# First attention's 16-tile matrix product by seven block products, and two of the down weights' block sums moved one layer later

## The chip, the cores and the metric

The kernel runs on one core of a Trainium2 chip. The metric is device time in microseconds (us) for one execution. A core has a matrix engine (TensorE, "PE" in the profile, with its weight loads as "PEld"), a vector engine (VectorE, "DVE"), an activation engine (ScalarE, "ACT"), a general engine (GpSimd, "POOL") and a queue engine that issues most of the transfers (SyncE, "SP"). Matrix products are written to eight banks of PSUM, each 128 partitions by 512 floats; everything else lives in SBUF.

## The reference

Four layers run one after the other on a token matrix x of 2048 by 1024, each on a layer norm of x and each added back to x: attention, gated unit, attention, gated unit. The weights of both attentions are the same, and so are those of both gated units.

```python
def _A_ref(x, wqkv, wo):                       # x is the layer-normed xn; 32 heads of 32
    q, k, v = split(x @ wqkv)                  # each 2048 x 1024
    pq, pk = phi(q), phi(k)                    # phi(t) = (t + 1 if t > 0 else exp(t)) + 1e-6
    kv = einsum("bhsd,bhse->bhde", pk, v)      # per head, sum over the 2048 tokens
    z = einsum("bhsd->bhd", pk)
    o = einsum("bhqd,bhde->bhqe", pq, kv) / (einsum("bhqd,bhd->bhq", pq, z)[..., None] + 1e-6)
    return o @ wo

def _B_ref(x, W_gate, W_up, W_down):           # F = 3584
    return (relu(x @ W_gate) * (x @ W_up)) @ W_down
```

Layer 0 and layer 2 are the attentions, layer 1 and layer 3 the gated units.

## The kernel before

v is never computed for the tokens. Since v = xn Wv, the kernel forms M = xnᵀ pk (1024 by 1024, a sum over all 2048 tokens) and multiplies Wv onto it afterwards, only on the diagonal blocks of the heads. The tokens are 16 tiles of 128. In layer 0 the product M is done plainly: 8 slices of 128 rows by 2 halves of 512 columns, each a chain of 16 matmuls over the token tiles.

```python
def m_units(d):                                       # layer 0, d = 0..7
    mt = self.temp([P, D], BF16, name=f"mt{l}_{d}")
    for h in range(H):                                # 2 halves
        ps = self.ps3.tile([P, NW], F32, tag="b")
        for t in range(self.ST):                      # 16 token tiles, L473
            nc.tensor.matmul(ps, lhsT=self.xn[l, t][:, d * P:(d + 1) * P],
                             rhs=self.pk[l, t][:, h * NW:(h + 1) * NW], ...)
            ...
        nc.scalar.activation(out=mt[:, h * NW:(h + 1) * NW], in_=ps, func=ACT.Copy)
        if h == H - 1:
            later.at(2, lambda: kv_step(d, mt))       # 8 matmuls of 128 columns (L485)
        later.tick()
```

In layer 2 the same M is done by Strassen's seven products in Winograd's form. M is split into 2 by 2 blocks of 512 by 512, with the tokens split into tiles 0 to 7 and 8 to 15. Each product is 4 PSUM banks of 8 matmuls (L534). The block sums are written over the tokens' own tiles, in float16.

```python
def m_products(q_first):                              # layer 2 only; cut
    X = [4 banks of pool ps, tag "a"]; Y = [2 of ps3, tag "b"] + [2 of kvp]
    def product(A, B, banks, start, done):
        for j in range(QT):                           # 4 banks
            for i in range(NS):                       # 8 token tiles, L534
                nc.tensor.matmul(banks[j], lhsT=A(i)[:, j * P:(j + 1) * P], rhs=B(i), ...)
            done(j)
            later.tick()
    product(lambda i: half(xn(i), 0), lambda i: half(pk(i), 0), X, True, lambda j: copy(Y[j], X[j]))
    product(lambda i: half(xn(NS + i), 0), lambda i: half(pk(NS + i), 0), X, False, evict(X, 0, 0))
    z_row()
    later.at(2, lambda: z_chain(0))
    ...
    product(lambda i: part(i, 0), lambda i: part(i, 2), V, True, keep)
    product(lambda i: part(i, 1), lambda i: part(i, 3), Y, False, lambda j: add(V[j], j))
    product(lambda i: f16(half(xn(NS + i), 0)), lambda i: half(pk(NS + i), 1), V, False, evict(V, 0, 1))
    product(lambda i: f16(half(xn(i), 1)), lambda i: f16(half(pk(i), 1)), Y, False, ...)
    ...                                               # copies, kv steps, then the o0 weights' load
    product(lambda i: half(xn(NS + i), 1), lambda i: f16(half(pk(NS + i), 0)), Y, False, last)
    q_first(); steps(1, 0); ring.load_to(ring.index((l, "o1")) + 1); finish_kv()
```

Around M: the k projections (`project`, L436) end just before it, each followed by `phi`: on ACT an exp, on DVE a `tensor_scalar` (L383) and a `scalar_tensor_tensor` (L385) that reads the projection's PSUM bank and frees it. The pk are summed over the tokens on POOL (L455). Beside and after M runs the chain of the denominators, token tile by token tile: multiply on POOL (L611), reduce and reciprocal on DVE (L616 to L618), scale on POOL (L623), transpose by a DMA on the SP queue (L628). After M come the last quarter's q projections, interleaved with four `fold_wo` (L642), which put kv and Wo together into T, and then the output product (L657) and the residual add (L664).

The gated units' weights are used by Strassen sums as well. Those of the down weights are made in layer 0 and stored in device memory for all four uses:

```python
for i in range(self.U // 2):                          # 7 pairs, from layer 0's second quarter on
    later.at(1 + 8 * i, lambda i=i: self.make_d(2 * i))
def make_d(self, u):                                  # load 1 MB; 6 turns later 4 DVE sums of
    ...                                               # 128x1024 (L806 to L809); then store 1 MB
```

The gate and up weights' sums are made in layer 1's first half (`make_gu`, L789 to L792), right behind the last multiply of a unit (`put`, L862). `later.at(n, f)` runs f after n turns, a turn being one matmul chain. `slot()` takes one of 16 SBUF buffers of 8 KB per partition.

Of the kernel before, what the change touches and what calls it, by code (L numbers as in the profile page):

```python
# [14 lines left out]
P = 128  # L15
NW = 512
HD = 32
QT = 4
# [71 lines left out]
class _Net:  # L90
# [146 lines left out]
    def head(self):  # L237
# [5 lines left out]
        nc.vector.memset(zero, 0.0)  # L243
        idle = self.ps3.tile([P, NW], F32, tag="b")
        for _ in range(11):
            nc.tensor.matmul(idle, lhsT=zero[:, 0:P], rhs=zero, start=True, stop=True)

# [122 lines left out]
    def phi(self, ps, out, kind):  # L370

        nc = self.nc
        e = self.temp()
        if kind == "v":
            nc.scalar.activation(out=e, in_=ps, func=ACT.Exp)
        else:
            nc.scalar.activation(out=e, in_=ps, func=ACT.Relu, scale=-1.0)
            nc.scalar.activation(out=e, in_=e, func=ACT.Exp, scale=-1.0)
            nc.scalar.activation(out=e, in_=e, func=ACT.Identity, bias=self.eps6[:, 0:1])

        def join():
            if kind == "v":
                nc.vector.tensor_scalar(out=e, in0=e, scalar1=1.0, scalar2=1e-6, op0=ALU.min,  # L383
                                        op1=ALU.add)
            nc.vector.scalar_tensor_tensor(out=out, in0=ps, scalar=0.0, in1=e,  # L385
                                           op0=ALU.max, op1=ALU.add)

        if self.phi_lag:
            self.later.at(self.phi_lag, join)
        else:  # L390
            join()
# [17 lines left out]
    def layer_A(self, l, last_ln):  # L409
# [4 lines left out]
        pq_of, pqT, T = {}, {}, []  # L414
        kv = [] if l else [self.kvp.tile([P, NW], F32, tag=f"kv{i}", name=f"kv{l}_{i}")
                           for i in range(H)]
        kvc = self.slot(f"kvc{l}", [P, 4, D])
# [23 lines left out]
        def k_unit(q, j, c, between=None):  # L441
# [4 lines left out]
            if l and t >= self.NS and c == H - 1:  # L446
                later.at(3, lambda: sums_k(t - self.NS))

# [18 lines left out]

        def m_units(d):
            mt = self.temp([P, D], BF16, name=f"mt{l}_{d}")
            for h in range(H):  # L470
                ps = self.ps3.tile([P, NW], F32, tag="b")
                for t in range(self.ST):
                    nc.tensor.matmul(ps, lhsT=self.xn[l, t][:, d * P:(d + 1) * P],  # L473
                                     rhs=self.pk[l, t][:, h * NW:(h + 1) * NW],
                                     start=(t == 0), stop=(t == self.ST - 1))
                    if t == self.ST // 2 - 1:
                        later.tick()
                nc.scalar.activation(out=mt[:, h * NW:(h + 1) * NW], in_=ps, func=ACT.Copy)
                if h == H - 1:
                    later.at(2, lambda: kv_step(d, mt))  # L480
                later.tick()

        def kv_half(d, mt, b):
# [6 lines left out]

        def kv_step(d, mt):
            for b in range(H):
                kv_half(d, mt, b)
            if d == KT - 1:
                ring.free_before((l, "q0"))
                finish_kv()

        half = lambda a, n: a[:, n * NW:(n + 1) * NW]
        part = lambda i, k: half(self.x[self.NS + i][:, :].bitcast(F16), k)
        sub = lambda out, a, b: nc.vector.tensor_tensor(out=out, in0=a, in1=b, op=ALU.subtract)  # L500

        def sums_n(i):

            a, b = self.xn[l, i], self.xn[l, self.NS + i]
            nc.vector.tensor_tensor(out=part(i, 0), in0=half(a, 1), in1=half(b, 1), op=ALU.add)
            sub(part(i, 1), part(i, 0), half(a, 0))
            sub(half(a, 1).bitcast(F16), half(a, 0), half(a, 1))

        def sums_k(i):
            a, b = self.pk[l, i], self.pk[l, self.NS + i]  # L510
            sub(part(i, 2), half(a, 1), half(a, 0))
            sub(part(i, 3), half(b, 1), part(i, 2))
            sub(half(a, 1).bitcast(F16), half(b, 1), half(a, 1))

        def sums_last(i):
            a, b = self.xn[l, self.NS + i], self.pk[l, self.NS + i]
            sub(half(a, 0).bitcast(F16), half(a, 0), part(i, 1))
            sub(half(b, 0).bitcast(F16), half(b, 0), part(i, 3))

        def m_products(q_first):  # L520

            NS = self.NS
            xn, pk = (lambda i: self.xn[l, i]), (lambda i: self.pk[l, i])
            f16 = lambda a: a.bitcast(F16)
            copy = lambda out, src: nc.scalar.activation(out=out, in_=src, func=ACT.Copy)
            X = [self.ps.tile([P, NW], F32, tag="a", name=f"mx{j}") for j in range(QT)]
            Y = [self.ps3.tile([P, NW], F32, tag="b", name=f"my{j}") for j in range(2)]
            Y += [self.kvp.tile([P, NW], F32, tag=f"kv{j}", name=f"my{2 + j}") for j in range(2)]
            mt, V, M5 = [], [], []

            def product(A, B, banks, start, done):
# [23 lines left out]
            z_row()  # L555
            later.at(2, lambda: z_chain(0))
            V += [self.ps.tile([P, NW], F32, tag="a", name=f"mv{j}") for j in range(QT)]
            for i in range(NS):
                later.at(1 + i // 2, lambda i=i: sums_last(i))
            product(lambda i: part(i, 0), lambda i: part(i, 2), V, True, keep)  # L560
# [69 lines left out]
        def fold_wo(n):  # L630
# [14 lines left out]
            for i in range(R):  # L645
                g = a * R + i
                dst = T[g // 4][:, g % 4, n2 * NW:(n2 + 1) * NW]
                if l or g % 2:
                    nc.scalar.activation(out=dst, in_=ps[i], func=ACT.Copy)
                else:  # L650
                    nc.vector.tensor_copy(out=dst, in_=ps[i])

# [34 lines left out]
        for i in range(QT, self.ST):  # L687
            self.ln_at((8 if l == 0 else 2) + 3 * (i - QT), l, i, 2)
            if l and i >= self.NS:
                later.at(4 + 3 * (i - QT), lambda i=i: self.send_away(i))  # L690
                later.at(10 + 3 * (i - QT), lambda i=i: sums_n(i - self.NS))
        if l == 0:
# [15 lines left out]
        for q in range(1, self.NQ - 1):  # L708
            if (l, q) == (0, 1):
                for i in range(self.U // 2):  # L710
                    later.at(1 + 8 * i, lambda i=i: self.make_d(2 * i))
            run(row_major(k_unit, q), row_major(q_unit, q))
        run(row_major(k_unit, self.NQ - 1))
        with self.tc.manual_schedule(engines={mybir.EngineType.DVE, mybir.EngineType.Pool}):
            q3 = row_major(q_unit, self.NQ - 1)
            out0 = column_major(out_unit, 0)
            if l == 0:
                ring.free_before((l, "v0"))
                later.at(5, z_row)
                later.at(7, lambda: z_chain(0))  # L720
                for d in range(KT):
                    m_units(d)
            else:
                ring.load_to(ring.index((l, "v1")) + 1)
                m_products(q3.pop(0))
                q3.insert(0, lambda: None)
                later.at(1, lambda: self.behind(ring.last, self.bring_back, range(self.NS)))
                for t in range(self.NS, self.ST, 2):
                    later.at(10 + t, lambda t=t: self.behind(self.last_turn, self.bring_back, (t, t + 1)))

# [53 lines left out]
    def make_gu(self, t, w, u):  # L784
# [9 lines left out]
            out=self.tgu[w, u], in_=t[:, 4:8, :].bitcast(F16)))  # L794

    def make_d(self, u):

        v = self.nc.vector
        t = self.slot(f"wd{u}", [P, 2, 4, NW])
        T = t[:, :, :, :].bitcast(F16)  # L800
        us = slice(u, u + 2)
        self.nc.sync.dma_start(out=t[:, :, :, :].rearrange("p u (h n) f -> p u h (n f)", h=2),
                               in_=self.wd_v[:, :, us, :].rearrange("p h u n -> p u h n"))

        def sums():
            v.tensor_tensor(out=T[:, :, 0, :], in0=t[:, :, 1, :], in1=t[:, :, 0, :], op=ALU.subtract)  # L806
            v.tensor_tensor(out=T[:, :, 1, :], in0=t[:, :, 3, :], in1=t[:, :, 1, :], op=ALU.subtract)
            v.tensor_tensor(out=T[:, :, 3, :], in0=t[:, :, 3, :], in1=T[:, :, 0, :], op=ALU.subtract)
            v.tensor_tensor(out=T[:, :, 2, :], in0=t[:, :, 2, :], in1=T[:, :, 3, :], op=ALU.subtract)  # L809
            self.later.at(2, lambda: self.nc.sync.dma_start(  # L810
                out=self.td[:, us, :, :], in_=T))

        self.later.at(6, sums)

# [155 lines left out]
    def layer_B(self, l, final):  # L970
# [6 lines left out]
        for c in range(2):  # L977
            hT = []
            first = l == 1 and c == 0
            for u in range(self.U):  # L980
                if u % 2 == 0:
                    hT.append(self.slot(f"h{l}_{c}_{u // 2}", dtype=F16))
                ring.load_to(ring.index((l, c, "g", u)) + 5)
                if first:
                    if u + 1 < self.U:
                        self.later.at(4, lambda u=u: behind(self.last_put if u else self.last_x, lambda: [
                            self.make_gu(ring.get((l, c, w, u + 1)), w, u + 1) for w in "gu"]))
                self.glu(l, c, u, hT)
                if c == 0 and u == (self.U - 1 if first else 0):
# [74 lines left out]
```

## Time and profile before

| what | value |
|---|---|
| time, median of three | 1479.12 us (1478.75 to 1479.19) |
| span of the profiled execution | 1476.4 us |
| PE busy / DVE busy / ACT busy / POOL busy | 1468.0 / 864.9 / 518.9 / 283.8 us |
| granted TensorE clock | 1.00 |
| layer 0's k and q projections | 9.5 to 105 us |
| layer 0's M product | 105.6 to 167 us |
| layer 1, first half, gated units | about 237 to 407 us |
| layer 2's M product | 841 to 895 us |

A line of the grouped view gives source line, engine, operation, written and read buffers with their shapes and the count; then the total busy time and the mean of one. A line of the view of stages gives the stretch, then for each engine its busy time and, in brackets, its count of instructions. A line of the timeline gives the start in us, the duration, and what ran; in square brackets how long the engine had been idle and what ended it.

### The profile page before, as it was taken

To read this page: it belongs to the slowest core of one execution; us is meant where nothing else is said; L and a number is where in the kernel's file an instruction comes from. 1 tells how busy PE (TensorE), PEld (TensorE's weight loads), DVE (VectorE), ACT (ScalarE), POOL (GpSimd) and SP (SyncE) were. 2 spreads that over 40 slices of the span, in tenths; PEclk is the share of its full clock that TensorE was granted. 3 is DMA by queue.
4 is the path that set the end of the run, shared out by engine and by line. 5 is a ranking of instruction groups with operands and counts; after the bars stand their busy time and mean duration, and the time that the engine had idled before them with its cause. 6 is when DMAs were issued, how large, how long until landed. Compare 5 with 4: busy or idle time off the path is not lost.

```text
span 1476.4 us, 18611 instructions
## 1 busy us (share of the span) xinstructions
PE 1468.0 (99%) x6965; PEld 667.7 (45%) x7007; DVE 864.9 (59%) x1487; ACT 518.9 (35%) x931; POOL 283.8 (19%) x190
## 2 busy tenths in 40 slices
PE   9999999999999999999999999999999999999999
PEld 4444444444444444444444444444444444444444
DVE  8995788666594433346379866874435434343632
ACT  5762323333330233340057525333333203333300
POOL 1356640111100011110023476401111001111000
PEclk9999999999999999999999999999999999999999
DMA  9856539444458953445933019994444688444461
GB/s 283 213 169 178 122 57 250 157 143 157 160 178 239 344 176 129 149 131 187 288 101 72 1 33 257 255 283 143 143 143 149 179 249 258 143 145 147 151 206 43
DMA packets 316060, 251.33 MB, mean 170 GB/s; under 512 B 105536, under 2 KB 291136, under 8 KB 315072
## 3 DMA queue, kind: packets, MB, share of 16 engines
q1 hardware_dynamic: 306000, 229.80, 53.0%
q10 hardware_dynamic: 9968, 20.32, 3.6%
q8 instruction: 55, 0.90, 0.3%
q14 instruction: 37, 0.30, 0.1%
HBM read 190.84 MB, written 34.60 MB: 153 GB/s over the span
## 4 chain that ended last, share of the span: by engine, by line
PE 91%; DVE 2%; issue 1%; ACT 0%; DVEq 0%
PE yg L851 10%; PE yu L851 10%; PE dy L935 10%; PE ps L436 8%; PE ps L657 7%; PE dv L935 7%; PE dx L935 7%; PE xu L851 6%; PE xg L851 6%; PE ps L473 4%; PE vg L851 3%; PE zu L851 3%; PE zg L851 3%; PE vu L851 3%; PE my L534 1%; PE mv L534 1%
## 5 line engine op out<-in xcount | busy, mean ns | idle before, releaser
L851 PEld LDWEIGHTS <-w 128*128 128x128 f16 (+1 forms) x3136 | 306.5, 98 | 370.9 <-DVE w L789 0.9
L889 POOL TENSOR_TENSOR h<-m5u,m5g 128x512 f16<-128x512 f32 x56 | 71.2, 1271 | 809.5 <-DVE m5u L885 798.6
L436 PE MATMUL ps<-w,xnT 128*128 128x512 bf16 x1024 | 223.9, 379 | 0.5 <-DVE pq L385 0.2
L935 PEld LDWEIGHTS <-h 128*128 128x128 f16 x1120 | 109.6, 98 | 132.1
L882 DVE TENSOR_TENSOR zg<-yg,m5g 128x512 f32<-128x512 f32 x56 | 39.1, 699 | 202.3 <-PE yg L851 202.3
L436 PEld LDWEIGHTS <-xnT 128*128 128x128 bf16 x1024 | 99.4, 98 | 120.9 <-issue 2.8
L851 PE MATMUL xu<-xnT,w 128*128 128x512 f16 x448 | 115.3, 379 | 0.0
L851 PE MATMUL xg<-xnT,w 128*128 128x512 f16 x448 | 115.1, 379 | 0.0
L851 PE MATMUL yu<-s,w 128*128 128x512 f16 x448 | 115.0, 379 | 0.0
L851 PE MATMUL yg<-s,w 128*128 128x512 f16 x448 | 115.0, 379 | 0.0
L657 PE MATMUL ps<-T,pqT 128*128 128x512 bf16 x500 | 110.4, 379 | 0.6
L859 ACT ACTIVATE m5g<-m5g 128x512 f32<-128x512 f32 x56 | 35.2, 629 | 199.7 <-DVE m5g L885 199.7
L935 PE MATMUL dy<-w,h 128*128 128x512 f16 x448 | 98.0, 379 | 0.0
L935 PE MATMUL dx<-w,h 128*128 128x512 bf16 x436 | 96.7, 379 | 0.6
L611 POOL TENSOR_TENSOR kvc<-pq,kvc 128x1024 f32<-128x1024 bf16 x32 | 70.6, 2206 | 70.3 <-DVE den L616 56.2
L161 ACT ACTIVATE rstd<-mv,eps 128x1 f32<-128x1 f32 x64 | 18.2, 290 | 169.6 <-DVE mv L159 169.5
L154 DVE BATCH_NORM_STATS2 stats<-x 128x6 f32<-128x512 f32 (+1 forms) x120 | 76.5, 671 | 1.9 <-DMA x<-in_A_x_dram 1.7
L657 PEld LDWEIGHTS <-pqT 128*128 128x128 bf16 x512 | 49.9, 98 | 60.4 <-issue 0.5
L455 POOL TENSOR_TENSOR kvc<-kvc,slab 128x512 f32<-128x512 f32 x46 | 58.3, 1274 | 75.1 <-DVE slab L385 57.4
L862 DVE TENSOR_TENSOR h<-yu,r 128x512 f16<-128x512 f32 x56 | 38.7, 691 | 56.1 <-PE yu L851 56.1
L885 DVE TENSOR_TENSOR m5u<-yu,m5u 128x512 f32<-128x512 f32 x56 | 38.7, 691 | 54.3 <-PE yu L851 53.3
L935 PEld LDWEIGHTS <-e 128*128 128x128 f16 x448 | 43.8, 98 | 52.9
(127 smaller groups left out, 1967.7 us busy)
## 6 DMA issues: line engine op xcount, KB each, us to landing
w<-in_B_W_gate_dram SPq DMA_DIRECT2D x56, 512.0 KB, 6.0
w<-in_B_W_up_dram SPq DMA_DIRECT2D x56, 512.0 KB, 4.6
w<-td SPq DMA_DIRECT2D x32, 896.0 KB, 4.8
w<-in_B_W_down_dram SPq DMA_DIRECT2D x24, 896.0 KB, 5.3
w<-tg SPq DMA_DIRECT2D x42, 512.0 KB, 7.0
w<-tu SPq DMA_DIRECT2D x42, 512.0 KB, 5.8
w<-in_A_wqkv_dram SPq DMA_DIRECT2D x10, 1024.0 KB, 8.1
away<-x SPq DMA_DIRECT2D x16, 512.0 KB, 4.0
```

The source lines that it names most:

```text
L154: self.nc.vector.bn_stats(out=stats[:, c, :], in_=src[:, c * fmax:(c + 1) * fmax])
L436: nc.tensor.matmul(by_row(ps), lhsT=self.xnT[l, l_q][:, kt, j * P:(j + 1) * P], rhs=w[:, kt, :].rearrange("p (b i d) -> p i b d", i=R, d=H ...
L455: nc.gpsimd.tensor_tensor(out=ksum[:, cols], in0=ksum[:, cols], in1=pk, op=ALU.add)
L473: nc.tensor.matmul(ps, lhsT=self.xn[l, t][:, d * P:(d + 1) * P], rhs=self.pk[l, t][:, h * NW:(h + 1) * NW], start=(t == 0), stop=(t == sel ...
L611: nc.gpsimd.tensor_tensor(out=prod, in0=pq_of[sc, j], in1=zrow, op=ALU.mult)
L657: nc.tensor.matmul(ps, lhsT=pqT[sc][:, g, j * P:(j + 1) * P], rhs=T[g // 4][:, g % 4, n2 * NW:(n2 + 1) * NW], start=(g == 0), stop=(g == G ...
L851: nc.tensor.matmul(ps, lhsT=W[w][m][:, k, :], rhs=A[m][:, k, :], start=start and k == 0, stop=k == 3, skip_group_check=True)
L862: self.last_put = nc.vector.tensor_tensor(out=h[:, b, :], in0=ps, in1=R.pop(b), op=ALU.mult)
L882: nc.vector.tensor_tensor(out=Z[w], in0=Y[w], in1=V[w], op=ALU.add)
L885: nc.vector.tensor_tensor(out=V[w], in0=Y[w], in1=V[w], op=ALU.add)
L889: nc.gpsimd.tensor_tensor(out=h[:, 3, :], in0=V["u"], in1=V["g"], op=ALU.mult)
L935: nc.tensor.matmul(banks[j], lhsT=A(k)[:, j * P:(j + 1) * P], rhs=w[:, i, :], start=start and k == 0, stop=k == self.U - 1, skip_group_che ...
```

## The change

Layer 0 now takes the route of layer 2: `m_units` is removed, and `m_products` serves both attentions. What differs in layer 0 is where the block sums live and when they are made. They are written over the raw tokens, which layer 0 holds as bf16 in the upper half of each x tile (`self.xb`); so the raw tokens are loaded from device memory once more before the output product adds them. The sums are made by 64 DVE operations of 128x512, four for each turn, beginning with M's first product.

```diff
-        def m_units(d): ...
+        def part(i, k):
+            if l == 0:
+                return half(f16(self.xb[self.NS + i if k < 2 else i]), k % 2)
+            return half(self.x[self.NS + i][:, :].bitcast(F16), k)
+        n1 = lambda i: op(part(i, 0), half(xn(i), 1), half(xn(self.NS + i), 1), ALU.add)
+        n2 = lambda i: op(part(i, 1), part(i, 0), half(xn(i), 0))
+        ...                                      # n3, n4, and k1 to k4 likewise
+            if l == 0:
+                jobs = [(f, i) for fs in ((n1, k1), (n2, k2), (n3, k3), (n4,), (k4,))
+                        for i in range(NS) for f in fs]
+                for n, (f, i) in enumerate(jobs):
+                    later.at(1 + n // 4, lambda f=f, i=i: f(i))
-            later.at(2, lambda: z_chain(0))
+            later.at(2 if l else 8, lambda: z_chain(0))
@@ layer_A
-            if l == 0:
-                ring.free_before((l, "v0"))
-                later.at(5, z_row)
-                later.at(7, lambda: z_chain(0))
-                for d in range(KT):
-                    m_units(d)
-            else: ...
+            bring = self.bring_back if l else self.load_x
+            ring.load_to(ring.index((l, "v1")) + 1)
+            m_products(q3.pop(0))
+            q3.insert(0, lambda: None)
+            later.at(1, lambda: self.behind(ring.last, bring, range(self.NS)))
+            for t in range(self.NS, self.ST, 2):
+                later.at(10 + t, lambda t=t: self.behind(self.last_turn, bring, (t, t + 1)))
```

Smaller parts go with it. The PSUM banks of pool kvp, which layer 0's kv held, become free for the products and for the warm-up matmuls at the start. `phi`'s intermediate becomes bf16 where DVE finishes it, in both attentions. All of `fold_wo`'s copies go to ACT. Two of the seven pairs of down weights' sums leave layer 0 and are made in layer 1's first half, one DVE operation in each of the units 2 to 9.

```diff
-        idle = self.ps3.tile([P, NW], F32, tag="b")
+        idle = [self.kvp.tile([P, NW], F32, tag=f"kv{i}", name=f"idle{i}") for i in range(2)]
@@ phi
-        e = self.temp()
+        e = self.temp(dtype=BF16 if kind == "v" else F32)
@@ fold_wo
-                if l or g % 2:
-                    nc.scalar.activation(out=dst, in_=ps[i], func=ACT.Copy)
-                else:
-                    nc.vector.tensor_copy(out=dst, in_=ps[i])
+                nc.scalar.activation(out=dst, in_=ps[i], func=ACT.Copy)
@@ layer_A
-                for i in range(self.U // 2):
+                for i in range(self.U // 2 - 2):
                     later.at(1 + 8 * i, lambda i=i: self.make_d(2 * i))
@@ layer_B, in the units of layer 1's first half
+                    if u in (1, 5):
+                        d = self.U - 4 + u // 2
+                        wd[d] = self.load_d(d)
+                    if 1 < u < 10:
+                        self.later.at(4, lambda d=self.U - 4 + (u - 2) // 4 * 2, n=(u - 2) % 4: behind(
+                            self.last_put, lambda: self.sums_d(wd[d], d, (n,))))
```

The change is for fewer matmuls in layer 0's M product, with the sums' work on an engine that has time there.

More of the change, by code (lines that the diff above doesn't have):

```diff
@@ L243, in head @@
         nc.vector.memset(zero, 0.0)
-        idle = self.ps3.tile([P, NW], F32, tag="b")
-        for _ in range(11):
-            nc.tensor.matmul(idle, lhsT=zero[:, 0:P], rhs=zero, start=True, stop=True)
+        idle = [self.kvp.tile([P, NW], F32, tag=f"kv{i}", name=f"idle{i}") for i in range(2)]
+        for i in range(11):
+            nc.tensor.matmul(idle[i % 2], lhsT=zero[:, 0:P], rhs=zero, start=True, stop=True)
         k0, k1, v0, q0, q1 = (ring.place() for _ in range(5))
@@ L414, in layer_A @@
         pq_of, pqT, T = {}, {}, []
-        kv = [] if l else [self.kvp.tile([P, NW], F32, tag=f"kv{i}", name=f"kv{l}_{i}")
-                           for i in range(H)]
+        kv = []
         kvc = self.slot(f"kvc{l}", [P, 4, D])
@@ L446, in k_unit @@
             if l and t >= self.NS and c == H - 1:
-                later.at(3, lambda: sums_k(t - self.NS))
+                later.at(3, lambda: sums(t - self.NS, k1, k2, k3))
         def k_sum(t, cols):
@@ L465, in z_row @@
                 nc.scalar.activation(out=zrow[:, i * NW:(i + 1) * NW], in_=ps, func=ACT.Copy)
[L468 to L481, printed above, removed]
         def kv_half(d, mt, b):
@@ L489, in kv_half @@
                                  skip_group_check=True)
[L491 to L496, printed above, removed]
-        half = lambda a, n: a[:, n * NW:(n + 1) * NW]
[L499 to L518, printed above, removed]
+        half = lambda a, n: a[:, n * NW:(n + 1) * NW]
@@ new lines, in layer_A, with op @@
+        f16 = lambda a: a.bitcast(F16)
+        xn, pk = (lambda i: self.xn[l, i]), (lambda i: self.pk[l, i])
+        def part(i, k):
+            if l == 0:
+                return half(f16(self.xb[self.NS + i if k < 2 else i]), k % 2)
+            return half(self.x[self.NS + i][:, :].bitcast(F16), k)
+        def op(out, a, b, how=ALU.subtract):
+            nc.vector.tensor_tensor(out=out, in0=a, in1=b, op=how)
+        n1 = lambda i: op(part(i, 0), half(xn(i), 1), half(xn(self.NS + i), 1), ALU.add)
@@ new lines, in layer_A @@
+        n2 = lambda i: op(part(i, 1), part(i, 0), half(xn(i), 0))
+        n3 = lambda i: op(f16(half(xn(i), 1)), half(xn(i), 0), half(xn(i), 1))
+        n4 = lambda i: op(f16(half(xn(self.NS + i), 0)), half(xn(self.NS + i), 0), part(i, 1))
+        k1 = lambda i: op(part(i, 2), half(pk(i), 1), half(pk(i), 0))
+        k2 = lambda i: op(part(i, 3), half(pk(self.NS + i), 1), part(i, 2))
+        k3 = lambda i: op(f16(half(pk(i), 1)), half(pk(self.NS + i), 1), half(pk(i), 1))
+        k4 = lambda i: op(f16(half(pk(self.NS + i), 0)), half(pk(self.NS + i), 0), part(i, 3))
@@ L520, in m_products, with sums @@
+        def sums(i, *fs):
+            for f in fs:
+                f(i)
         def m_products(q_first):
             NS = self.NS
-            xn, pk = (lambda i: self.xn[l, i]), (lambda i: self.pk[l, i])
-            f16 = lambda a: a.bitcast(F16)
             copy = lambda out, src: nc.scalar.activation(out=out, in_=src, func=ACT.Copy)
@@ L555, in m_products @@
             z_row()
-            later.at(2, lambda: z_chain(0))
+            later.at(2 if l else 8, lambda: z_chain(0))
             V += [self.ps.tile([P, NW], F32, tag="a", name=f"mv{j}") for j in range(QT)]
-            for i in range(NS):
-                later.at(1 + i // 2, lambda i=i: sums_last(i))
+            if l:
+                for i in range(NS):
+                    later.at(1 + i // 2, lambda i=i: sums(i, n4, k4))
             product(lambda i: part(i, 0), lambda i: part(i, 2), V, True, keep)
@@ L690, in layer_A @@
                 later.at(4 + 3 * (i - QT), lambda i=i: self.send_away(i))
-                later.at(10 + 3 * (i - QT), lambda i=i: sums_n(i - self.NS))
+                later.at(10 + 3 * (i - QT), lambda i=i: sums(i - self.NS, n1, n2, n3))
         if l == 0:
@@ L716, in layer_A @@
             out0 = column_major(out_unit, 0)
-            if l == 0:
-                ring.free_before((l, "v0"))
-                later.at(5, z_row)
-                later.at(7, lambda: z_chain(0))
-                for d in range(KT):
-                    m_units(d)
[L723 to L729, printed above, removed]
+            bring = self.bring_back if l else self.load_x
[5 more added lines that the diff above has]
+                later.at(10 + t, lambda t=t: self.behind(self.last_turn, bring, (t, t + 1)))
             def with_fold(u, i):
@@ L794, in make_gu, with load_d, sums_d @@
             out=self.tgu[w, u], in_=t[:, 4:8, :].bitcast(F16)))
-    def make_d(self, u):
[L798 to L813, printed above, removed]
+    def load_d(self, u):
+        t = self.slot(f"wd{u}", [P, 2, 4, NW])
+        self.nc.sync.dma_start(out=t[:, :, :, :].rearrange("p u (h n) f -> p u h (n f)", h=2),
+                               in_=self.wd_v[:, :, u:u + 2, :].rearrange("p h u n -> p u h n"))
+        return t
+    def sums_d(self, t, u, ops=range(4)):
+        T = t[:, :, :, :].bitcast(F16)
+        for n in ops:
+            out, a, b = ((T[:, :, 0, :], t[:, :, 1, :], t[:, :, 0, :]),
+                         (T[:, :, 1, :], t[:, :, 3, :], t[:, :, 1, :]),
+                         (T[:, :, 3, :], t[:, :, 3, :], T[:, :, 0, :]),
+                         (T[:, :, 2, :], t[:, :, 2, :], T[:, :, 3, :]))[n]
+            self.nc.vector.tensor_tensor(out=out, in0=a, in1=b, op=ALU.subtract)
+            if n == 3:
+                self.later.at(2, lambda: self.nc.sync.dma_start(
+                    out=self.td[:, u:u + 2, :, :], in_=T))
+    def make_d(self, u):
+        t = self.load_d(u)
+        self.later.at(6, lambda: self.sums_d(t, u))
     def sums_x(self, l, c, j):
@@ L979, in layer_B @@
             first = l == 1 and c == 0
+            wd = {}
             for u in range(self.U):
```

## The prediction

> **What bounds the kernel now.** I read the page's busy times first, then the chain that ended last, then the stages, then the timelines of layer 2's M product, which already is what layer 0's is to become. From the page:
>
> ```profile
> PE 1468.0 (99%) x6965; PEld 667.7 (45%) x7007; DVE 864.9 (59%) x1487; ACT 518.9 (35%) x931; POOL 283.8 (19%) x190
> ...
> PE 91%; DVE 2%; issue 1%; ACT 0%; DVEq 0%
> ```
>
> PE holds 91% of the chain, and the span of 1476.4 us has 8.4 us in which PE is not busy. So hardly anything can be won from waits. Time comes out only with matmuls taken away, and goes in with every wait that the change opens. The Trainium skill, "Perfetto Trace Analysis", section Identifying the Most-Contended Engine, warns that a busy matmul row is no measure of how near the peak one is; the records here say the same (a matmul's record is 379 ns long, but the next one starts after 216). I therefore count instructions and use spacings.
>
> The stages (start and end; then PE, PEld, DVE, ACT, POOL busy with counts; clock; DMA share; GB/s):
>
> ```profile
> 95.00:109.00 14.00, 13.72 (x63) 6.17 (x63) 13.60 (x19) 4.18 (x7) 8.43 (x7) 1.00 0.36 123
> 109.00:165.00 56.00, 55.46 (x294) 26.99 (x300) 31.65 (x42) 11.10 (x19) 43.91 (x24) 1.00 0.55 150
> 165.00:180.00 15.00, 15.00 (x118) 6.57 (x117) 12.57 (x21) 8.09 (x15) 5.20 (x3) 1.00 0.81 206
> 237.00:407.00 170.00, 169.86 (x786) 76.55 (x785) 104.75 (x188) 65.09 (x112) 17.81 (x14) 1.00 0.51 168
> 832.00:845.00 13.00, 12.84 (x59) 5.78 (x59) 12.27 (x19) 4.17 (x7) 7.10 (x7) 1.00 0.00 1
> 845.00:893.00 48.00, 47.90 (x257) 23.24 (x258) 29.44 (x52) 13.04 (x22) 35.47 (x18) 1.00 0.18 33
> ```
>
> Layer 0's M (second row) and layer 2's (last row) both keep PE full; the seven-product route costs PE no wait to speak of. DVE is half idle in both. Only just before M is DVE the tighter engine (13.60 of 14 us).
>
> **The saving.** Layer 2's products in the PE timeline:
>
> ```profile
> 855.62 7.07 PE L534 MATMUL mv<-x 128*128 128x512 f16 x32
> 862.52 7.07 PE L534 MATMUL my<-x 128*128 128x512 f16 x32
> ```
>
> 32 matmuls in float16 from start to start are 862.52 - 855.62 = 6.90 us, 0.2157 us each. "TensorE: Matmul & The Clock Gate", section Back-to-back issue gap, gives 518 cycles at 2.4 GHz for 512 columns, 216 ns; the trace agrees. (The same section's 131 ns for a sustained stream is nowhere in this trace.) Layer 0 has 8 slices x 2 halves x 16 tiles = 256 such matmuls, and will have 7 products x 4 banks x 8 tiles = 224. Gone are 32 x 0.2157 = **6.9 us**. The kv steps stay at 64 matmuls and the row of sums at 2. As a check on whole stages: layer 0's M runs from 105.58 to 166.97, less one q unit of 1.73 that lies inside it, 59.7 us; layer 2's from 841.11 to 895.45, less 1.72, 52.6 us. The difference, 7.1 us, has in it some waits of layer 0.
>
> **The 64 sums on DVE.** Layer 2's own, from the DVE and POOL timelines:
>
> ```profile
> 845.93 1.76 DVE L500 TENSOR_TENSOR x<-slab,x 128x512 f16<-128x512 bf16 x2
> 853.88 5.45 DVE L500 TENSOR_TENSOR slab<-slab,x 128x512 f16<-128x512 bf16 x16 [6.18 <-PE mx L534]
> ```
>
> ```profile
> 844.92 2.50 POOL L455 TENSOR_TENSOR kvc<-kvc,slab 128x512 f32<-128x512 f32 x2 [1.56 <-DVE slab L385]
> 857.10 4.21 POOL L611 TENSOR_TENSOR kvc<-pq,kvc 128x1024 f32<-128x1024 bf16 x1 [9.69 <-ACT kvc L465]
> ```
>
> Sixteen sums in a row take 5.45 us, 0.34 each. Beside a POOL operation a sum takes 0.88, and the POOL multiply takes 4.21 beside the sums instead of the 2.12 of its fellows. "VectorE: DVE Perf Modes", section The perf-mode tier table, has tensor_tensor on 16-bit data in SBUF at two elements per cycle, and "SBUF — State Buffer", section Who interferes with whom, has GpSimd and a DVE instruction with two SBUF inputs share a read port; both agree with these lines. Hence I take 0.34 us when POOL is idle and 0.88 when it is not. The timing chain, with M starting at 105.3:
>
> - DVE finishes the k projections' phi at 110.5 (last L385 at 109.78, 0.69 long), and perhaps 1 us sooner with bf16: L383 takes 0.41 alone in float32, for which the same tier table has two elements per cycle, against four in bf16. POOL's sums of pk end at 111.8. So two sums at 0.88 and fourteen at 0.34 put n1 and k1 at about 117. The third product, their first reader, starts at 105.3 + 2 x 6.9 + 0.4 = 119.5. Margin 2.5 us.
> - n2, k2 end at 122.5; the fourth product starts at 126.4. Margin 4 us.
> - n3, k3 end at 128. Then DVE works in order through add, four of n4, add, four of n4, the adds at some 0.65 us and held by the fourth product's banks (128.1, 129.9): n4 ends near 132.3. The fifth product starts at 133.3. Margin 1 us, the smallest.
> - k4 comes after that, read only from 147 on.
>
> The chain of the denominators, which would put POOL beside the sums, begins late enough: 8 turns after the second product are just the end of the fourth, 133. So all 64 sums, 22 us of DVE time, lie beside matmuls; on the path **0 us**, at worst 1 us at the fifth product.
>
> **What moves.** The denominators' chain begins at 133 instead of 116 and takes POOL's 3.95 us for each tile (L611 from 150.19 to 154.13), so eleven tiles end near 179. The output product begins at about 174 and then needs only tiles 0 to 3 (transposed by 156), tiles 4 to 7 at 187 (there by 172), 8 to 11 at 201. Hidden. But DVE gets the chain's 2.15 us per tile beside the last q projections: eight times 0.69 and about 0.4, four to five tiles, and one copy of kv are 19 us in the 16 that those projections with their folds take, less what the fold copies no longer ask of it (they were 4 x 1.28). The four PSUM banks in front let DVE lag by some 5 us. I put 0.3 us.
>
> The o0 weights were loaded at 107.86 and now are asked for in the seventh product, near 150, behind transposes on the same queue. In layer 2 they were issued at 893.25 and the fold began at 899.06, with nothing to spare and PE at 16.00 of 16 us. An estimate for the same in layer 0 is 0 to 2 us of waiting; I put 0.3.
>
> The M product's first four banks are now the pool that the k projections use. Each is free only when L385 has read it. The last four reads end at 105.6, 108.1, 109.2 and 110.5, and PE wants banks at 105.3, 107.0, 108.8, 110.5. That is a wait of some 1 us, against which a wait of 0.46 goes away:
>
> ```profile
> 109.23 5.56 PE L473 MATMUL ps<-slab,x 128*128 128x512 bf16 x25 [0.46 <-DVE slab L385]
> ```
>
> With bf16 in L383 the reads come a little earlier; net **+0.2 us**.
>
> The two pairs of down weights' sums in layer 1: eight operations of 128x1024, 0.6 us each in a row. They go behind the multiply that ends a unit, where these already are:
>
> ```profile
> 276.00 0.75 DVE L792 TENSOR_TENSOR w<-w 128x512 f16<-128x512 bf16 x2
> 278.48 0.70 DVE L882 TENSOR_TENSOR zg<-yg,m5g 128x512 f32<-128x512 f32 x1 [1.73 <-PE yg L851]
> ```
>
> DVE idles 1.73 us there in each unit, and 0.6 fits. Their transfers (4 MB) meet a DMA share of 0.51. Cost 0. In layer 0 they were on DVE at 118 to 122 and 131 to 137, where PE did not wait for it. The second loading of x is 16 x 256 KB in a stretch of low share: 0.
>
> Sum: 1479.1 - 6.9 + 0.3 + 0.3 + 0.2 = **1473.0 us**, 0.4% faster.
>
> **Rivals.** First, *the sums come too late*: DVE can't keep the margins, because POOL's tail or the phi lag eats them, and PE waits at products three to five. For it: margins of 1 to 4 us out of a DVE queue that is full until 110, and operations that lengthen from 0.34 to 0.88. Against: the delayed chain and layer 2's stage without a wait. It would give back 2 to 5 us: 1475 to 1478. Second, *the end of M is held up*: by o0, by finish_kv's copy behind the reduces in DVE's order, or by SBUF buffers. M holds two more of the 16 (kvc 1, pk 4, xnT 1, pq 4, weights 4, and now M itself 2, which makes 16), so that the first transposed tile waits for pk's release after the sixth product. Layer 2 has the same count. It would cost 1 to 4 us: 1474 to 1477. Third, *the saving is hidden*, because another engine bounds the stage: against it stands PE's 55.46 of 56 us; it would leave 1479. Fourth, *more than the matmuls*: DVE relieved before M and at the head also takes away waits; all the waits of PE up to 180 are about 3 us, so at most 1 us more, 1471.5.
>
> **Range and chances.** The floor is the count of matmuls less a little, 1471; the top is one rival in full, 1476.5. I put the range at 1470.8 to 1476.5. Two per cent are 29.6 us. No part of the change can bring that, and only a wait in every unit of layer 1 could cost it. So: faster by over 2% 0.01, within 2% 0.98, slower by over 2% 0.01.
>
> **What would show it.** Right: in layer 0's M, seven groups of 32 matmuls 6.9 us apart, the stage at 52 to 53.5 us, hardly a wait of PE for a sum; the sums near 0.34 us; layer 1's first half still 169 to 170 us; layers 2 and 3 as they were. Wrong: PE waiting for sums before the third or fifth product (first rival), for a weight, T or kvc at the folds (second rival), units of layer 1 longer than 12.1 us, or a shift in layers 2 and 3 that only phi's bf16 can have brought.

## The result, and the profile after

The changed kernel takes 1483.75 us (median of six, 1483.35 to 1486.05), beside 1478.29 us for the kernel before in the same runs. The ratio is 1.0041, with a 95% interval of 1.0028 to 1.0054: it is **slower by 0.4%**, where 1473.0 us and 0.4% faster were predicted. The profiled span went from 1476.4 to 1481.5 us.

From the page of the kernel after:

```profile
PE 1464.6 (99%) x6975; PEld 664.5 (45%) x6975; DVE 880.9 (59%) x1551; ACT 525.3 (35%) x943; POOL 285.2 (19%) x190
...
PE 88%; DVE 3%; POOL 1%; DMA 0%; issue 0%; SPq 0%; ACT 0%; DVEq 0%
```

The span less PE's busy time was 8.4 us and is now 16.9. PE's share of the chain fell from 91 to 88%. The same stages as before the prediction, after the change:

```profile
95.00:109.00 14.00, 11.43 (x52) 4.97 (x51) 13.42 (x22) 4.56 (x8) 6.84 (x6) 1.00 0.34 119
109.00:165.00 56.00, 54.20 (x286) 25.74 (x284) 37.40 (x72) 14.73 (x25) 28.60 (x17) 1.00 0.21 58
165.00:180.00 15.00, 14.38 (x121) 6.60 (x120) 13.27 (x17) 9.23 (x19) 11.95 (x6) 1.00 0.75 229
180.00:237.00 57.00, 52.54 (x257) 23.50 (x255) 53.02 (x101) 16.96 (x31) 29.97 (x15) 1.00 0.77 163
237.00:407.00 170.00, 169.91 (x787) 76.52 (x785) 110.20 (x198) 63.36 (x109) 16.52 (x13) 1.00 0.62 202
845.00:893.00 48.00, 48.00 (x241) 22.46 (x240) 31.06 (x56) 13.08 (x23) 32.98 (x18) 1.00 0.16 28
```

The holes are in the first row, just before M, and in the fourth, where the output product begins; layer 1 and layer 2 are as full as they were. Fixed points of the PE timeline make a balance of it. M is taken from its first matmul to the q projection behind the last kv step, less the one q unit inside; layer 1 from its first matmul.

| stretch | before | after | difference |
|---|---|---|---|
| start to M's first matmul | 105.58 | 110.18 | +4.60 |
| M | 59.66 | 54.65 | -5.01 |
| M's end to layer 1 (q projections, folds, output product) | 69.22 | 74.88 | +5.66 |
| layer 1 to the end | 1240.2 | 1240.1 | -0.1 |

So all of it happens in layer 0. M became shorter, with the products that read the sums 6.9 us apart as predicted (126.71, 133.62, 140.53, 147.43), and two stretches that the change hardly touches by its text gave back twice that. The first hole, in PE's timeline after:

```profile
101.63 3.61 PE L435 MATMUL ps<-w,xnT 128*128 128x512 bf16 x16 [1.24 <-DVE slab L385]
105.50 1.89 PE L435 MATMUL ps<-w,xnT 128*128 128x512 bf16 x8 [0.26 <-DVE slab L385]
108.46 1.89 PE L435 MATMUL ps<-w,xnT 128*128 128x512 bf16 x8 [1.07 <-DVE slab L385]
110.18 1.89 PE L517 MATMUL mx<-slab,x 128*128 128x512 bf16 x8
112.93 1.89 PE L517 MATMUL mx<-slab,x 128*128 128x512 bf16 x8 [0.85 <-DVE slab L385]
```

PE waits for L385, the phi operation that frees a PSUM bank. Two more such waits, of 1.22 and 0.69 us, end at 87.25 and 91.56. And this is DVE just before M:

```profile
102.60 0.55 DVE L485 TENSOR_TENSOR x<-slab,x 128x512 f16<-128x512 bf16 x1
103.08 1.37 DVE L485 TENSOR_TENSOR x<-x,x 128x512 f16<-128x512 f16 x1
104.37 0.28 DVE L383 TENSOR_SCALAR e<-e 128x512 bf16<-128x512 bf16 x1
104.76 0.69 DVE L385 SCALAR_TENSOR_TENSOR slab<-ps,e 128x512 bf16<-128x512 f32 x1
...
110.70 1.24 DVE L383 TENSOR_SCALAR e<-e 128x512 bf16<-128x512 bf16 x1
111.86 0.41 DVE L485 TENSOR_TENSOR x<-slab,x 128x512 f16<-128x512 bf16 x1
112.20 0.68 DVE L385 SCALAR_TENSOR_TENSOR slab<-ps,e 128x512 bf16<-128x512 f32 x1
```

L485 are the block sums. They do not wait for M: 27 of the 64 stand before M's first matmul, the first at 67.3 us, among the phi operations of the k and q projections; 23 of them run before 95 us. Some take 0.4 us, some 1.38, and L383 takes 0.28 or 1.24.

The second hole begins with the last q projections. PE, then DVE and POOL for one round of their pattern:

```profile
185.18 3.80 PE L638 MATMUL ps<-T,pqT 128*128 128x512 bf16 x16 [2.01 <-DVE pq L385]
191.36 48.94 PE L638 MATMUL ps<-T,pqT 128*128 128x512 bf16 x226 [2.38 <-DVE pq L385]
```

```profile
180.78 1.21 DVE L600 TENSOR_REDUCE den<-kvc 128x32 f32<-128x1024 f32 x1
182.02 0.18 DVE L601 TENSOR_SCALAR den<-den 128x32 f32<-128x32 f32 x1
182.23 0.35 DVE L602 RECIPROCAL den<-den 128x32 f32<-128x32 f32 x1
182.50 1.82 DVE L383 TENSOR_SCALAR e<-e 128x512 bf16<-128x512 bf16 x1
184.43 0.69 DVE L385 SCALAR_TENSOR_TENSOR pq<-ps,e 128x512 bf16<-128x512 f32 x1
185.04 1.20 DVE L383 TENSOR_SCALAR e<-e 128x512 bf16<-128x512 bf16 x1
186.35 0.69 DVE L385 SCALAR_TENSOR_TENSOR pq<-ps,e 128x512 bf16<-128x512 f32 x1
186.96 1.21 DVE L600 TENSOR_REDUCE den<-kvc 128x32 f32<-128x1024 f32 x1
```

```profile
182.06 2.12 POOL L595 TENSOR_TENSOR kvc<-pq,kvc 128x1024 f32<-128x1024 bf16 x1 [2.15 <-DVE den L600]
184.14 1.96 POOL L607 TENSOR_TENSOR pq<-pq,den 128x1024 bf16<-128x1024 bf16 x1
```

The first L383 ends at 184.32, just as POOL's multiply does (184.18); the second ends at 186.24, just after POOL's scale (186.10). One round is 186.96 - 180.78 = 6.18 us for two q units, and PE needs 2 x 1.73 and a fold of 0.4 for them, 3.9. DVE falls back by 2.3 us in each round, until the banks in front are used up.

### The profile page after: what moved, and what is told of

It reads as the page before. It is cut to its first block, busy times and chain, and to the rows that moved or that the text cites. A ratio compares the mean times of both kernels' runs of the same rounds, so it can differ in the third digit from the quotient of the medians.

```text
span 1481.5 us, 18698 instructions
## 1 busy us (share of the span) xinstructions
PE 1464.6 (99%) x6975; PEld 664.5 (45%) x6975; DVE 880.9 (59%) x1551; ACT 525.3 (35%) x943; POOL 285.2 (19%) x190
## 4 chain that ended last, share of the span: by engine, by line
PE 88%; DVE 3%; POOL 1%; DMA 0%; issue 0%; SPq 0%; ACT 0%; DVEq 0%
PE yg L830 10%; PE yu L830 10%; PE dy L914 10%; PE ps L435 7%; PE ps L638 7%; PE dv L914 7%; PE dx L914 7%; PE xu L830 6%; PE xg L830 6%; PE vg L830 3%; PE vu L830 3%; PE zu L830 3%; PE zg L830 3%; PE my L517 2%; PE mx L517 2%; PE mv L517 1%
## 5 line engine op out<-in xcount | busy, mean ns | idle before, releaser
L914 PEld LDWEIGHTS <-h 128*128 128x128 f16 x1120 | 109.6, 98 | 132.1
```

The source lines that it names most:

```text
L914: nc.tensor.matmul(banks[j], lhsT=A(k)[:, j * P:(j + 1) * P], rhs=w[:, i, :], start=start and k == 0, stop=k == self.U - 1, skip_group_che ...
```

## The experiments

The theory after the result: two separate losses. **First**, the sums are placed among the phi operations and delay them, so that M starts late. **Second**, the chain of denominators, begun later, stands beside the last q projections, where phi's `tensor_scalar` waits for POOL's operations. The rivals: bf16 in phi, the down sums moved to layer 1, the fold copies on ACT, the o0 weights or the reload of x. The ratios are to the kernel before, timed beside; they are not the ratios of the medians and can differ a little from them.

**Sums behind the last phi of the k projections.**

```diff
-                    later.at(1 + n // 4, lambda f=f, i=i: f(i))
+                    later.at(1 + n // 4, lambda f=f, i=i, it=self.last_join: self.behind(it, f, (i,)))
```

`last_join` is the last phi operation (L385) issued before M, and `behind` lets a sum be issued only after it.

> The changed kernel, with layer 0's 64 block sums put behind the last phi operation of the k projections on DVE (they had been placed among them). Theory (the sums delay the phi operations that free PSUM, so M starts late): M starts at 105 to 106 us instead of 110.2, its first product loses its three waits, and the time falls by 5 to 6.5 us to about 1477.5; the waits after M stay. Rival (bf16 phi or the moved down sums delay the phi operations): M still starts near 109 to 110, the time stays within 1.5 us of 1483.7, or rises because the sums now come late to products three to five.

Measured: 1476.12 us, ratio 0.9994 (0.9985 to 1.0002). M starts at 105.02 and takes 52.36 us. All 64 sums are inside M, and PE's timeline shows no wait there:

```profile
105.02 13.98 PE L517 MATMUL mx<-slab,x 128*128 128x512 bf16 x62
118.83 0.59 PE L462 MATMUL ps<-e,ones 128*128 128x512 bf16 x2
119.26 7.07 PE L517 MATMUL mv<-x,x 128*128 128x512 f16 x32
126.17 7.07 PE L517 MATMUL my<-x,x 128*128 128x512 f16 x32
```

The first loss is the placing of the sums; it is worth 5.2 us before M and 2.3 inside it. The stretch after M did not shorten but grew to 76.57 us. DVE's pace sets it: from M's end to the end of PE's last wait it is 24.8 us in both kernels. The remaining 1.7 us come behind that wait in this profiled execution, and are told below.

**Chain of denominators early again.**

```diff
-            later.at(2 if l else 8, lambda: z_chain(0))
+            later.at(2, lambda: z_chain(0))
```

> The changed kernel, with layer 0's chain of denominators started 2 turns after the second product, as in layer 2, instead of 8. Theory (the late chain puts POOL and the reduces beside the last q projections, where phi's DVE operation waits for POOL): the 5 us of PE waits from 178 to 192 go, the stretch from M's end to layer 1's start falls from 78.4 to 73 to 74 us, time about 1479; up to 1 us may come back in products three to five. Rival (fold copies on ACT, the o0 load, or the reload of x hold the stretch): it stays at 77 to 79 us and the time within 1.5 us of 1483.7.

(The expectation counts the stretch from an earlier point than the table does.) Measured: 1485.69 us, ratio 1.0051 (1.0036 to 1.0066). The stretch after M did fall, from 74.88 to 71.21 us, and the waits for phi in it all but vanished. But M grew from 54.65 to 59.97. The expectation missed what the chain does among the sums; the next one shows it without the first loss.

**Both edits.**

> Both of the first two edits. If the two losses are separate and complete, they add: time 1472 to 1473.5, layer 1 starting near 233 us. If something else holds a part, less than the sum of both gains comes; if the early chain's POOL work slows the sums that are now all inside M, products three to five wait, and the time is 1474 to 1477.

Measured: 1481.47 us, ratio 1.0027 (1.0017 to 1.0037). M starts at 104.92 but takes 59.67 us. DVE, POOL and PE in it:

```profile
129.62 4.10 DVE L485 TENSOR_TENSOR x<-x 128x512 f16<-128x512 bf16 x4
...
137.90 4.09 DVE L485 TENSOR_TENSOR slab<-slab,x 128x512 f16<-128x512 bf16 x4
```

```profile
128.60 2.13 POOL L595 TENSOR_TENSOR kvc<-pq,kvc 128x1024 f32<-128x1024 bf16 x1 [1.33 <-DVE den L600]
130.68 2.10 POOL L607 TENSOR_TENSOR pq<-pq,den 128x1024 bf16<-128x1024 bf16 x1
```

```profile
142.66 3.21 PE L517 MATMUL mv<-slab,x 128*128 128x512 bf16 x8 [2.73 <-DVE mv L531]
```

Four sums take 4.1 us instead of 1.4, as the first two must wait until POOL is done at 132.8; the add that PE waits for until 142.66 stands behind the second such row. So the late start of the chain is needed by the sums, and costs at the other end. After M PE also waits 2.64 us for kv's copy, which now stands behind a reduce and a slow L383: a piece of the prediction's second rival. The gains do not add; this falls on the expectation's last clause, and worse than its 1474 to 1477.

**Half of the last q projections' phi on ACT.**

```diff
-                     "s" if sc < self.NQ - 1 or (l and j < 2) else "v")
+                     "s" if sc < self.NQ - 1 or j < 2 else "v")
```

> The changed kernel, with phi of half of layer 0's last q projections done on ACT as in layer 2 (no tensor_scalar on DVE for those). Theory (DVE with POOL in front is the bound there): four tensor_scalar of 1.2 to 1.8 us leave DVE, the stretch from M's end to layer 1 falls by 3 to 5 us, time about 1479.5. Rival (loads or folds hold the stretch): no change.

Measured: 1483.73 us, ratio 1.0040 (1.0026 to 1.0054); the stretch after M takes 73.63 us, a gain of 1.2 and not of 3 to 5. In layer 0 these units' three ACT operations stand beside the fold copies, half of which the change has moved there, so phi's results for them came late, and the four units left to DVE still had 1.2 to 1.8 us each. This run alone does not tell the theory from its rivals. The next two do.

**Without the denominators' work.** Layer 0's first eleven token tiles go undivided into their transposes.

```diff
-            z_mult(*divmod(i, QT))
+            if l:
+                z_mult(sc, j)
+            else:
+                self.last_turn = nc.sync.dma_start_transpose(...)   # pq as it is
```

> The kernel with the sums behind (first experiment), and for layer 0's first eleven token tiles the multiply, reduce, reciprocal and scale of the denominators left out: their pq goes into its transpose undivided. Theory (phi's DVE operations wait for that chain's POOL work and stand behind its reduces): the 7.3 us that the stretch after M is longer than before go almost all, layer 1 starts near 229 us instead of 235.7, time about 1469. Rival (o0 load, reload of x, fold copies on ACT): layer 1 still starts at 234 or later.

Measured: 1470.49 us, ratio 0.9951 (0.9933 to 0.9969), with that work left out. The stretch after M takes 69.22 us, to the hundredth what it took before the change. Loads, folds and the reload of x, all still there, cost nothing. L383 in the stretch of 155 to 192 us, without and (second fence, 159 to 192 us, the kernel with the sums behind) with the chain:

```profile
L383 DVE TENSOR_SCALAR e<-e 128x512 bf16<-128x512 bf16 x8 | 2.3, 294 | 17.7 <-ACT e L375 17.7
```

```profile
L383 DVE TENSOR_SCALAR e<-e 128x512 bf16<-128x512 bf16 x8 | 11.5, 1444 | 1.2 <-ACT e L375 1.2
```

Of the 11.5 us, 9.2 are waiting. But this run also takes away the reduces in front of them, with their reciprocals 1.7 us per tile in the round shown above, so it does not yet say which of the two is the loss.

**Phi without the shared port.** The same function, to within the 1e-6 beside 1 for positive q, by max(q, 1e-6) + exp(min(q, 0)), whose minimum reads PSUM.

```diff
+        elif kind == "p":                      # layer 0's last q projections
+            nc.vector.tensor_scalar(out=e, in0=ps, scalar1=0.0, scalar2=None, op0=ALU.min)
+            nc.scalar.activation(out=e, in_=e, func=ACT.Exp)
@@ join, two turns later
-            nc.vector.scalar_tensor_tensor(out=out, in0=ps, scalar=0.0, in1=e,
+            nc.vector.scalar_tensor_tensor(out=out, in0=ps, scalar=1e-6 if kind == "p" else 0.0, in1=e,
```

> The kernel with the sums behind, and in layer 0's last q projections the DVE minimum taken from the projection's PSUM bank ahead of the exponential, in place of the one from SBUF behind it; nothing left out. Theory (it is the wait for POOL, not the amount of DVE work): each such operation takes its own 0.68 us and never 1.2 or 1.8, DVE keeps up to within 2 us, layer 1 starts at 229 to 231, time 1469 to 1471. Rival (the amount of DVE work in that stretch is too much whatever its form): layer 1 starts at 233 or later, time above 1473.

Measured: **1470.51 us, ratio 0.9953** (0.9937 to 0.9968), with nothing left out. M 52.34 us, the stretch after it 69.62. DVE's groups there:

```profile
L377 DVE TENSOR_SCALAR e<-ps 128x512 f32<-128x512 f32 x8 | 5.4, 681 | 0.6 <-PE ps L438 0.6
L388 DVE SCALAR_TENSOR_TENSOR pq<-ps,e 128x512 bf16<-128x512 f32 x8 | 5.2, 648 | 0.0
```

An operation that by itself is more than twice as long (0.68 against 0.29 us), in the same units and beside the same POOL and reduce work, takes the loss away. So it was the wait for POOL, not the amount of DVE work. The edit also puts this operation ahead of the exponential and the join two turns later, which was not tried alone; but with the sums behind DVE waited for the exponential only 1.2 us in all, while the eight operations became 11.5 - 5.4 = 6.1 us shorter. This version beats both kernels.

**Phi's intermediate in float32 again**, with the sums behind.

```diff
-        e = self.temp(dtype=BF16 if kind == "v" else F32)
+        e = self.temp()
```

> The kernel with the sums behind, and phi's intermediate in float32 again as before the change. If bf16 itself brings the long waits for POOL: the stretch after M shortens by 3 us or more and the time falls to about 1473. If both forms wait for POOL alike: within 1 us of the first experiment, with L383 near 0.41 us where POOL is idle and 1.2 to 1.8 where it is not.

Measured: 1479.03 us, ratio 1.0009 (1.0002 to 1.0016). It is slower than with bf16, not faster: M starts 0.66 us later and waits 0.6, the stretch after M takes 77.50 us, and L383 there has a mean of 1.58 us. bf16 is no cause of the loss; both forms wait for POOL, and bf16 is some 2 us to the good in the whole, more than the 1 us that was expected.

**The small parts alone**, on the kernel before: phi in bf16, fold copies on ACT, two pairs of down sums in layer 1.

> The kernel before, with the small parts of the change alone: phi's intermediate in bf16, all fold copies on ACT, two pairs of down sums moved to layer 1; layer 0's M stays plain. Theory (the small parts cost nothing): within 1 us of before, at best 0.5 us faster from the relieved k projections. Rival (the moved sums or ACT's fold copies cost something): slower by 1 us or more, and then the stage says where.

Measured: 1476.67 us, ratio 0.9995 (0.9987 to 1.0004). M starts at 105.22, M loses its 0.46 us wait, the stretch after it takes 69.23. They cost nothing.

**The second repair alone.**

> The changed kernel with the second repair alone (minimum from PSUM in layer 0's last q projections), the sums left where they were placed. If the two losses are separate: M still starts near 110 us with its three waits, the stretch from M's end to layer 1 falls from 74.9 to about 69.5 us, layer 1 starts near 236, time 1477.5 to 1478.5, level with before. If the second loss hangs on the first: less than 4 us of gain.

Measured: 1479.79 us, ratio 1.0013 (1.0004 to 1.0022). The stretch after M falls to 69.62 us as expected; M starts at 111.51 with the three waits of the changed kernel. The two losses are separate. The time is 1.5 us above before in place of level, which is about how much later M starts here than in the changed kernel (1.3 us). Of that, 1.13 us are one more wait of PE for a q projection's phi, ending at 80.18; why the order on DVE came out so, the runs do not tell.

## Why the prediction was wrong, step by step

- *"Gone are 32 x 0.2157 = 6.9 us."* Right. With the sums behind, M takes 52.36 us against 59.66: 7.3, of which 0.46 is the wait that went.
- *"All 64 sums, 22 us of DVE time, lie beside matmuls; on the path 0 us."* **This step failed first.** It took for granted that DVE begins them when the k projections' phi is done. The edit asks for them with M's first product, but no operation on DVE held them there: their inputs were ready, and 27 came in front of M. In place of 0 they cost 5.2 us before M and 2.3 inside it. The prediction called the 14 us before M the only stretch where DVE is the tighter engine (13.60 us, though PE has 13.72 in the same row), and left out the row before it, which 23 of the 27 went into, also with a full DVE (kernel before):

```profile
20.00:95.00 75.00, 74.63 (x345) 33.58 (x344) 71.51 (x127) 56.26 (x112) 26.13 (x21) 1.00 0.82 227
```

  Between 60 and 105 us DVE idles some 5 us without the sums, and the 27 took 18. The chain of margins itself held once the sums were put behind: n4 was expected to end near 132.3 and ended at 132.1, and no product waited.
- *"I put 0.3 us"* for the denominators' chain beside the last q projections. **This step failed second: 5.7 us in place of 0.3.** (It is 7.3 with the sums behind, of which 1.7 are the slow matmuls told below.) The term that was mis-sized is the "about 0.4" for L383. It had 1.44 on average: POOL works for 4.1 us in each round of 6.2, and starts when the reduce right in front of the two L383 is done. My own fence of layer 2's sums showed the effect, 0.88 for 0.34, and I used it for the sums only. Before the change the chain was over at 170.8, three units into these projections, but the two L383 that fell beside it already had 1.38 and 0.96 us, the six behind it 0.41 to 0.43:

```profile
167.41 1.38 DVE L383 TENSOR_SCALAR e<-e 128x512 f32<-128x512 f32 x1 [0.96 <-ACT e L375]
170.09 0.96 DVE L383 TENSOR_SCALAR e<-e 128x512 f32<-128x512 f32 x1
```

- *PSUM banks in front of M, net +0.2 us.* With the sums behind, PE's first product has no wait: 0.
- *o0 weights, 0.3 us*: no wait for them in any run. *Down sums in layer 1, 0*: right; from its first matmul to its down product layer 1's first half takes 405.99 - 236.19 = 169.80 us before and 411.23 - 241.43 = 169.80 after. *Reload of x, 0*: right.
- The first rival had the sums too late; they were too early. The second named DVE's order at M's end, but for kv's copy, the loads and the buffers, not for phi; kv's copy held PE only where the chain began early (0.96 and 2.64 us). With both losses mended the kernel is at 1470.5, 7.0 us faster than the one timed beside it, where the prediction's matmul count alone gives 6.9. That these two numbers meet is partly chance: between the profiled executions M gains 7.3 us and its start 1.1, and the stretch after it loses 0.4.

## What to carry to other kernels

Work that is meant to hide in an idle stretch must be tied to that stretch: if its inputs are ready early and nothing on its engine holds it back, look in the timeline at where it was really placed, and above all whether that is in front of the operation that frees the bottleneck's buffers. When a chain on POOL is moved, go through every DVE operation that will run beside it, and take its time from a row where POOL was busy. A longer form of an operation that reads PSUM can be the faster one there.

## What the runs showed of the hardware that was not expected

**POOL and DVE hold each other up in both directions.** "SBUF — State Buffer", section Who interferes with whom, says that whoever issues first has the shared ports for the whole instruction; here a DVE operation of 0.29 us stands for 1.82 us until POOL's ends (182.50 in the second hole above). But a row of DVE sums 0.34 us apart keeps POOL out as well: with the sums behind, the chain's first multiply, 2.12 us elsewhere, took

```profile
120.75 6.61 POOL L595 TENSOR_TENSOR kvc<-pq,kvc 128x1024 f32<-128x1024 bf16 x1 [11.09 <-ACT kvc L464]
```

from 120.75 to the end of the sums' row at 125.4, and then its own time. The operations that read PSUM and one SBUF tensor (L385, 0.63 to 0.69 us in layer 0 of every run) were never held.

**A wait can leave the matmuls slow behind it.** In the profiled execution of the kernel with the sums behind, PE's waits of 2.02 and 2.38 us are followed by weight loads 0.43 us apart, twice the usual, for nine matmuls:

```profile
184.56 0.15 PEld L638 LDWEIGHTS <-pqT 128*128 128x128 bf16 x1 [0.28 <-issue]
184.99 0.15 PEld L638 LDWEIGHTS <-pqT 128*128 128x128 bf16 x1 [0.28 <-issue]
185.42 0.15 PEld L638 LDWEIGHTS <-pqT 128*128 128x128 bf16 x1 [0.27 <-issue]
```

The granted clock from 183.9 to 187.5 us is 0.53, though the mean of the span reads 0.999. That is the 1.7 us by which its stretch after M is longer than the changed kernel's, where equal waits (2.01 and 2.38) left none. This execution took 1478.02 us, 1.9 more than the median, so most executions probably lack it. "TensorE: Matmul & The Clock Gate", section What's actually happening, has a gate that halves the clock after an idle window of some 3.4 us that runs freely. The doubled spacing agrees. But here shorter waits were enough: 2.0 and 2.4 us with 4 us of matmuls between in one run and not in another, and 2.65 and 2.73 us inside M in the two runs with the early chain (clock 0.64 and 0.59 in the 3 us or so behind). That the free-running window decides which is a guess from that page; no run here tests it.
